# Score operands of a pair's first entry loaded in one transfer, and the issue time of a transfer counted in the list schedule

## The chip, the cores and the metric

The kernel runs on one core of one Trainium2 chip. The time is what the device takes for one execution, in microseconds (us), and lower is better. TensorE does the matrix products, VectorE, ScalarE and GpSimd the elementwise work (PE, DVE, ACT and POOL in the rows), and SyncE (SP) issues every transfer between HBM and SBUF.

## The reference

Three stages follow one another, all in float32:

```python
# attention: q, k, v are [4, 8, 576, 64]
scores = scale * np.matmul(q, k.transpose(0, 1, 3, 2))
mask = block_i >= block_j                 # blocks of 64 positions
scores = np.where(mask, scores, -1000000000.0)
scores = scores - np.max(scores, axis=-1, keepdims=True)
attn = np.exp(scores)
attn = attn / (np.sum(attn, axis=-1, keepdims=True) + 1e-09)
attn_out = np.matmul(attn, v)
x = attn_out.transpose(0, 2, 1, 3).reshape(2304, 512)
# first feed-forward, w1..w3 [512, 768], w_out [768, 512]
x = np.maximum(np.maximum(x @ w1, x @ w2), x @ w3) @ w_out
# second, w_in [512, 2048], w_out [2048, 512]
h = np.maximum(x @ w_in, 0.0)
return h * h @ w_out
```

## The kernel before

**Work and tiles.** Two heads of a batch entry make a pair, so there are 16 pairs of which the first `NPAIR` = 4 are batch entry 0. The 576 queries of a pair are cut into two groups, `GROUPS = ((0, 256), (256, 320))`. For the first four pairs the group 0 entries (256 queries, 256 keys) are done first, all four pairs, then the group 1 entries. An entry goes: score matmuls `sc` from the query tile and the key tile, the block mask and row maximum `nm` on DVE, the exponential `P` with its row sum on ACT, transposes `tp`, copies `ta`/`tb`, matmuls with `v` (`av`), row sums `r`, and the split of the result into a high and a low part (`xh`, `xl`) from which the feed-forward multiplies in three products. For the first entries the score operands are float32: for pair n a tile `zk` of 128 partitions x 3 x 256, made of two zero-padded query planes (one per head, from `in_z`) and the keys (from `in_k`). The tag `tb` of `zk` has two buffers, so the third pair's `zk` takes the buffer of the first.

**Weights.** Weight chunks of 128 x 512 float64 words come in as `raw_w`, `raw_wo`, `raw_wi` (512 KB each). ACT, DVE and POOL turn each into float32 and split it into a high and a low part (`w1h`/`w1l`, `wo1h`/`wo1l`, `wos`, and `wq` out of `wqf`). For the last feed-forward the kernel writes prepared weights back to HBM (`wo_d`, `wq_d`) and loads them again per pass (`wol`/`woh`, `wq`); `ys` tiles are written to `y_d` and come back as `yf`. In the last stage `up` makes seven products per step in two banks (`ph_x`, `ph_y`, six matmuls each), ACT copies the first of them out as `p`, DVE forms `c`, ACT and DVE split it into `g`, and `down` adds into six banks (`acc`), nine matmuls for each `g`.

**What sets the order.** Nothing is issued as the code is read. `Plan.note` records each operation with its dependences and a rank, and `Plan.issue` is a list scheduler: for each engine it keeps a time at which it is free, takes the operation that can start earliest (lowest rank first), gives it a length from `duration` or `transfer`, and emits it. The order on every engine, SP's included, comes out of those modelled times; on the chip each engine then runs its list in that order and waits in it. All emitted instructions carry the line of `Plan.call`, L187. `Plan.issue` runs twice: once for attention, the first feed-forward of the early batches and the preparation of `wo_d`, and once for the rest.

**The model's cost of a transfer.** An instruction on SP made SP busy for 60 ns, and its transfer ended at a modelled queue time plus 400 ns.

**Names.** `score_operands_f32` loads the score operands of an entry, `prefetch` calls it, and `kernel` lays out the arrays in HBM. The profile names a transfer by its tile and its source, as `zk<-in_z`.

## Time and profile before

| | us |
|---|---|
| median of 3 runs (lowest to highest) | 888.12 (883.44 to 889.05) |
| the profiled execution | 888.7 |
| its span, first to last instruction | 886.9 |
| PE busy | 864.2 (97% of the span) |
| DVE busy | 601.1 (68%) |
| ACT busy | 424.9 (48%) |
| POOL busy | 104.0 (12%) |

The profiled execution is one run, 0.6 us above the median, and 1.8 us of it lie outside the span. Busy times are shares of the whole span, over stages with different limits; a row of a timeline gives the start, the length, the engine, the operation with its tile and sources, and in brackets how long the engine stood idle ahead of it and what released it.

### The profile page before, as it was taken

The numbers are of one execution on the slowest core, as the hardware profiler recorded it, in microseconds if no ns is written. First come the engines' busy times: TensorE is split into PE (matmuls) and PEld (weight loads), VectorE is DVE, ScalarE is ACT, GpSimd is POOL, SyncE is SP. The second block draws the span as 40 slices with busy tenths as digits, with TensorE's granted clock in tenths as the row PEclk, the third lists the DMA queues.
The fourth block names the chain that finished last, engine by engine and source line by source line (L and its number), as shares of the span: only waits on it lengthen the run. The fifth ranks groups of instructions, "written<-read, shape, count | busy, mean of one in ns | idle before, by whom it ended". The sixth has DMA issues, their size and how long they took to land.

```text
span 886.9 us, 14852 instructions
## 1 busy us (share of the span) xinstructions
PE 864.2 (97%) x5464; PEld 777.7 (88%) x5464; DVE 601.1 (68%) x1376; ACT 424.9 (48%) x1016; POOL 104.0 (12%) x94
## 2 busy tenths in 40 slices
PE   5899999999999999999999989999999999999997
PEld 4567799998999989899999979898999989999896
DVE  6998678878788988646557766546755457544543
ACT  6888667667688787544555231113211114211111
POOL 2233200000001111214442230000000000000000
PEclk9999999999999999999999999999999999999999
DMA  8745432232255563554656578454765536655221
GB/s 294 237 138 174 131 114 89 85 115 86 85 184 177 175 213 118 196 190 165 257 203 237 164 299 338 160 230 168 270 229 184 207 145 229 215 200 196 72 72 71
DMA packets 52056, 157.73 MB, mean 178 GB/s; under 512 B 8592, under 2 KB 16016, under 8 KB 48400
## 3 DMA queue, kind: packets, MB, share of 16 engines
q1 hardware_dynamic: 51984, 156.78, 50.5%
q8 instruction: 43, 0.70, 0.3%
q14 instruction: 29, 0.24, 0.1%
HBM read 124.26 MB, written 32.51 MB: 177 GB/s over the span
## 4 chain that ended last, share of the span: by engine, by line
PE 92%; DVE 2%; DMA 2%; ACT 2%; issue 0%; POOL 0%; SPq 0%; ACTq 0%; POOLq 0%; DVEq 0%
PE l L187 34%; PE acc L187 22%; PE ph_x L187 11%; PE ph_y L187 8%; PE av L187 5%; PE sc L187 5%; PE tp L187 4%; PE sc_t L187 2%; DMA raw_wi<-in_win 1%; PE tp_t L187 1%; DMA raw_wo<-in_wo 1%; DMA zk<-in_k 1%; PE r L187 0%; ACT P L187 0%; DVE f_wo L187 0%
## 5 line engine op out<-in xcount | busy, mean ns | idle before, releaser
L187 PE MATMUL acc<-woh,g 128*128 128x512 f32 x576 | 198.5, 395 | 0.0
L187 PE MATMUL l<-xh,w1l 128*128 128x256 f32 (+1 forms) x576 | 174.3, 303 | 0.9 <-DVE run L187 0.9
L187 PE MATMUL l<-xl,w1h 128*128 128x256 f32 (+1 forms) x576 | 172.2, 299 | 0.0
L187 PE MATMUL l<-xh,w1h 128*128 128x256 f32 (+1 forms) x576 | 172.2, 299 | 0.0
L187 ACT CAST g<-c 128x384 fp32r<-128x384 f32 x96 | 49.3, 513 | 220.8 <-DVE c L187 220.8
L187 PEld LDWEIGHTS acc<-woh,g 128*128 128x128 f32 x576 | 108.5, 189 | 19.4
L187 PE MATMUL acc<-wol,g 128*128 128x512 f32 x288 | 113.3, 393 | 0.0
L187 PEld LDWEIGHTS l<-xh,w1l 128*128 128x128 f32 x576 | 109.0, 189 | 4.1 <-issue 1.5
L187 PEld LDWEIGHTS l<-xl,w1h 128*128 128x128 f32 x576 | 109.1, 189 | 2.6 <-issue 1.7
L187 PEld LDWEIGHTS l<-xh,w1h 128*128 128x128 f32 x576 | 109.1, 189 | 1.9 <-issue 1.2
L187 PE MATMUL ph_x<-t,wq 128*128 128x384 f32 x432 | 87.7, 337 | 2.7 <-ACT p L187 2.7
L187 PEld LDWEIGHTS ph_x<-t,wq 128*128 128x128 f32 x432 | 77.4, 188 | 8.9 <-ACT p L187 3.1
L187 DVE TENSOR_TENSOR g<-c,g 128x384 fp32r<-128x384 f32 x96 | 53.6, 560 | 43.0 <-ACT g L187 42.6
L187 ACT ACTIVATE P<-sc,nm 128x128 f32<-128x128 f32 (+3 forms) x128 | 66.9, 530 | 9.9 <-DVE nm L187 8.4
L187 DVE TENSOR_TENSOR run<-l,run 128x256 f32<-128x256 f32 (+1 forms) x96 | 43.7, 455 | 27.9 <-PE l L187 26.3
L187 POOL TENSOR_TENSOR f_wo<-f_wo,raw_wo 128x512 int32<-128x512 int32 x22 | 29.8, 1357 | 276.5 <-DVE sm L187 180.3
L187 PEld LDWEIGHTS acc<-wol,g 128*128 128x128 f32 x288 | 54.3, 189 | 7.8
L187 PE MATMUL l<-hh,wo1l 128*128 128x256 f32 (+1 forms) x192 | 57.7, 306 | 2.2 <-DVE wo1l L187 2.1
L187 PE MATMUL ph_y<-b,wq 128*128 128x384 f32 x288 | 58.3, 337 | 0.0
L187 PE MATMUL l<-hl,wo1h 128*128 128x256 f32 (+1 forms) x192 | 57.5, 301 | 0.0
L187 PE MATMUL l<-hh,wo1h 128*128 128x256 f32 (+1 forms) x192 | 57.4, 300 | 0.0
L187 DVE TENSOR_REDUCE nm<-sc 128x2 f32<-128x256 f32 (+2 forms) x96 | 55.1, 588 | 0.8
(135 smaller groups left out, 1613.1 us busy)
## 6 DMA issues: line engine op xcount, KB each, us to landing
wq<-wq_d SPq DMA_DIRECT2D x20, 1792.0 KB, 8.6
wq_d<-wq SPq DMA_DIRECT2D x8, 1792.0 KB, 7.7
raw<-in_qk SPq DMA_DIRECT2D x24, 576.0 KB, 3.8
wol<-wo_d SPq DMA_DIRECT2D x48, 256.0 KB, 3.2
woh<-wo_d SPq DMA_DIRECT2D x48, 256.0 KB, 4.8
raw_wo<-in_wo SPq DMA_DIRECT2D x22, 512.0 KB, 3.8
raw_w<-in_w SPq DMA_DIRECT2D x18, 512.0 KB, 5.0
wo_d<-wos SPq DMA_DIRECT2D x16, 512.0 KB, 3.1
```

The source lines that it names most:

```text
L187: return getattr(engine, op_name)(*map(value, args), **{k: value(x) for k, x in kw.items()})
```

## The change

Two things change. The three transfers of a first entry's score operands (`z` of head 0, `k`, `z` of head 1; 128 KB each) become one transfer of 384 KB from a new array `zk0` that `kernel` lays out in the tile's own order, for each of the four first pairs; before, the sources were rows of 1 KB, now they are rows of 3 KB. In the scheduler, issuing a transfer now holds SP for 430 ns in place of 60, and a transfer that starts in the first 6 us of the modelled time is counted 1.4 times as long. The number of transfers falls by eight; no arithmetic changes.

```diff
--- before.py
+++ after.py
@@ -264,9 +264,9 @@
                 held[e] = t + length - HOLD[e]
             for other in op.engines:
                 del waiting[other][i]
-            if e == "sp":
-                queue = max(t + 1500, queue) + transfer(op)
-                op.end, free[e] = queue + 400, t + 60
+            if op.name == "dma_start":
+                queue = max(t + 1500, queue) + transfer(op) * (1.4 if t < 6000 else 1)
+                op.end, free[e] = queue + 400, t + 430
             else:
                 op.end = t + length
                 free[e] = op.end - LAP[e]
@@ -345,7 +345,7 @@
 
 
 @with_exitstack
-def fused_kernel(ctx: ExitStack, tc: tile.TileContext, z0, k0, qk, v, w123, wo1, win2, wo2, out):
+def fused_kernel(ctx: ExitStack, tc: tile.TileContext, z0, zk0, k0, qk, v, w123, wo1, win2, wo2, out):
     nc = Plan(tc)
     mm = nc.tensor.matmul
 
@@ -493,9 +493,12 @@
         else:
             z = [at.tile([128, w], F32, tag=t, bufs=CFG["QB"][2 * (t == "kl")], name=f"z{n}_{t}") for t in ("qs", "kl")]
             k = at.tile([128, S], F32, tag="kh", bufs=CFG["QB"][1], name=f"k{n}")
-        nc.sync.dma_start(out=z[0], in_=z0[n, :, 0, a:a + w])
-        nc.sync.dma_start(out=k, in_=k0[n, :, :a + w])
-        nc.sync.dma_start(out=z[1], in_=z0[n, :, 1, a:a + w])
+        if n < NPAIR and g == 0:
+            nc.sync.dma_start(out=zk, in_=zk0[n])
+        else:
+            nc.sync.dma_start(out=z[0], in_=z0[n, :, 0, a:a + w])
+            nc.sync.dma_start(out=k, in_=k0[n, :, :a + w])
+            nc.sync.dma_start(out=z[1], in_=z0[n, :, 1, a:a + w])
         return [[(z[h], k)] for h in range(2)], None
 
     def value_operands(n, g):
@@ -1020,6 +1023,8 @@
         z0[:, h, :, h] = qn[:, h]
     z0, k0 = z0.reshape(PAIRS, 128, 2, S), kn.reshape(PAIRS, 128, S)
 
+    zk0 = np.stack([z0[:NPAIR, :, 0, :GA], z0[:NPAIR, :, 1, :GA], k0[:NPAIR, :, :GA]], axis=2)
+
     qk = np.stack([a.transpose(0, 2, 1, 3) for a in (qn, kn)], axis=3)
     qk = np.concatenate([qk, qk], axis=1)
 
@@ -1035,7 +1040,7 @@
     w123 = w123.reshape(NC1, 128, 3 * KC * 128)
     win2 = w["moe2_w_in"].reshape(KC, 128, NC2, 128).transpose(2, 1, 0, 3).reshape(NC2, 128, KC * 128)
     arrays = {
-        "z0": z0, "k0": k0, "qk": qk, "v": vc, "w123": w123, "wo1": w["moe_w_out"], "win2": win2, "wo2": w["moe2_w_out"],
+        "z0": z0, "zk0": zk0, "k0": k0, "qk": qk, "v": vc, "w123": w123, "wo1": w["moe_w_out"], "win2": win2, "wo2": w["moe2_w_out"],
     }
     arrays = {f"in_{n}": np.ascontiguousarray(a) for n, a in arrays.items()}
```

Since the scheduler's times changed, the instructions on all engines come in another order. Below, L187 is the line all have and the number behind a name counts tiles in the program, so it differs between the versions.

On ACT, at the very start, the float exponentials `P` of the first pair and the first pass over the first weight chunk `raw_w_0_0`. Before:

```order
L187 ACTIVATE raw_w_0_0_86<-raw_w_0_0_86 128x512
L187 ACTIVATE P_0_0_138,sm_0_139<-sc_0_0_120,nm_0_127 128x128 x2
L187 ACTIVATE P_1_0_149,sm_0_139<-sc_1_0_122,nm_1_135 128x256 x2
L187 ACTIVATE raw_w_0_0_86<-raw_w_0_0_86 128x512
L187 ACTIVATE raw_w_0_1_94<-raw_w_0_1_94 128x512
L187 COPY ta_158<-tp_1_0_161 128x2x256
L187 ACTIVATE raw_w_0_1_94<-raw_w_0_1_94 128x512
L187 CAST w1h_188<-raw_w_0_0_86 128x512
```

and now:

```order
L187 ACTIVATE P_0_0_119,sm_0_120<-sc_0_0_100,nm_0_110 128x128 x2
L187 ACTIVATE raw_w_0_0_84<-raw_w_0_0_84 128x512
L187 ACTIVATE P_1_0_135,sm_0_120<-sc_1_0_105,nm_1_122 128x256 x2
L187 ACTIVATE raw_w_0_0_84<-raw_w_0_0_84 128x512
L187 COPY ta_143<-tp_1_0_148 128x2x256
L187 COPY rs_0_172<-r_0_165 128x256
L187 CAST w1h_174<-raw_w_0_0_84 128x512
L187 ACTIVATE P_0_0_186,sm_0_187<-sc_0_0_151,nm_0_162 128x128 x2
```

The first pair's first exponentials (`P_0_0`) moved ahead of the weight chunk, and the second pair's (`P_0_0_186`) ahead of the second weight chunk.

On SP, the loads ahead of the third pair's `zk` (`zk_129` before, `zk_124` now). Before:

```order
L187 DMA raw_w_1_1_100<-in_w 128x1024
L187 DMA z_qs<-in_z 128x320
L187 DMA k_104<-in_k 128x576
L187 DMA z_kl<-in_z 128x320
L187 DMA z_qs<-in_z 128x320
L187 DMA k_110<-in_k 128x576
L187 DMA z_kl<-in_z 128x320 x2
L187 DMA kt_116<-in_k 128x576
L187 DMA zt_118<-in_z 128x2x64
L187 DMA zk_129<-in_z 128x256
L187 DMA zk_129<-in_k 128x256
L187 DMA zk_129<-in_z 128x256
```

and now:

```order
L187 DMA raw_w_1_1_96<-in_w 128x1024
L187 DMA z_qs<-in_z 128x320
L187 DMA k_102<-in_k 128x576
L187 DMA z_kl<-in_z 128x320
L187 DMA z_qs<-in_z 128x320
L187 DMA k_116<-in_k 128x576
L187 DMA zk_124<-in_zk 128x768
L187 DMA z_kl<-in_z 128x320 x2
L187 DMA kt_137<-in_k 128x576
L187 DMA zt_141<-in_z 128x2x64
L187 DMA zk_179<-in_zk 128x768
L187 DMA v_0_189<-in_v 128x256
```

The third pair's operands moved ahead of two `z_kl` loads, `kt` and `zt`; the fourth pair's (`zk_179`) stay behind them.

On SP, near the start of the last stage, the loads of the last two weight chunks `raw_wi`, which stand behind the loads of prepared weights `wol`/`woh`. Before:

```order
L187 DMA wol_1_6701<-wo_d 128x512
L187 DMA woh_1_6705<-wo_d 128x512
L187 DMA wol_9_6708<-wo_d 128x512
L187 DMA woh_9_6712<-wo_d 128x512
L187 DMA wq_d<-wq_6387 128x3584
L187 DMA y_d<-ys_1_3_6724 128x320
L187 DMA raw_wi_6753<-in_win 128x1024
L187 DMA raw_wi_6784<-in_win 128x1024
```

now, first the rows ahead of the `wol`/`woh` loads:

```order
L187 DMA raw_wi_6374<-in_win 128x1024
L187 DMA wq_d<-wq_6372 128x3584
L187 DMA yf_0_6531<-y_d 128x2x768
L187 DMA yf_1_6612<-y_d 128x2x768
L187 DMA y_d<-ys_1_0_6645 128x320
L187 DMA y_d<-ys_1_1_6655 128x320
L187 DMA wol_0_6682<-wo_d 128x512
```

and then the rows up to the same chunks:

```order
L187 DMA woh_1_6709<-wo_d 128x512
L187 DMA wol_1_6717<-wo_d 128x512
L187 DMA y_d<-ys_1_3_6715 128x320
L187 DMA woh_9_6726<-wo_d 128x512
L187 DMA wol_9_6733<-wo_d 128x512
L187 DMA raw_wi_6738<-in_win 128x1024
L187 DMA raw_wi_6757<-in_win 128x1024
```

The 1792 KB write `wq_d<-wq` that stood two rows ahead of the chunks now stands ahead of the `yf` loads; eight `wol`/`woh` loads stand ahead of the chunks in both.

On ACT, in the same place, from the first copy `p` of the last stage to the second. Before:

```order
L187 COPY p_0_0_6737<-ph_0_x 128x384
L187 CAST g_0_0_0_6763<-c_0_00_6750 128x384
L187 CAST wq_6782<-wqf_6717 128x3x256
L187 CAST g_0_1_1_6806<-c_0_11_6794 128x384
L187 CAST wq_6782<-wqf_6717 128x4x256
L187 CAST g_0_0_1_6831<-c_0_01_6812 128x384
L187 ACTIVATE raw_wi_6753<-raw_wi_6753 128x512
L187 ACTIVATE wqf_6846<-raw_wi_6753 128x512
L187 ACTIVATE wqf_6846<-raw_wi_6784 128x512
L187 CAST g_0_1_0_6860<-c_0_10_6828 128x384
L187 COPY p_0_1_6865<-ph_1_x 128x384
```

and now:

```order
L187 COPY p_0_0_6729<-ph_0_x 128x384
L187 CAST wq_6755<-wqf_6450 128x3x256
L187 CAST g_0_0_0_6762<-c_0_00_6744 128x384
L187 CAST wq_6755<-wqf_6450 128x4x256
L187 ACTIVATE raw_wi_6738<-raw_wi_6738 128x512
L187 ACTIVATE raw_wi_6757<-raw_wi_6757 128x512
L187 CAST g_0_1_1_6807<-c_0_11_6787 128x384
L187 ACTIVATE wqf_6816<-raw_wi_6738 128x512
L187 ACTIVATE wqf_6816<-raw_wi_6757 128x512
L187 CAST g_0_0_1_6825<-c_0_01_6804 128x384
L187 CAST g_0_1_0_6842<-c_0_10_6821 128x384
L187 COPY p_0_1_6848<-ph_1_x 128x384
```

The first pass over both `raw_wi` chunks moved ahead of three of the four `g` splits of the first step; before, one split (`g_0_1_0`) and the copy `p_0_1` stood behind them.

## Rows read from the trace of the kernel before

**Rows 1.** The span in stretches: busy us of each engine, granted clock, DMA.

```profile
0.00:12.00 12.00, 6.49 (x21) 5.08 (x22) 4.06 (x13) 4.97 (x13) 1.99 (x7) 1.00 0.82 273
12.00:25.00 13.00, 8.42 (x59) 5.33 (x57) 12.11 (x28) 10.63 (x27) 4.21 (x3) 1.00 0.96 319
25.00:50.00 25.00, 22.94 (x159) 14.94 (x159) 24.53 (x68) 23.21 (x65) 8.26 (x6) 1.00 0.70 224
...
100.00:110.00 10.00, 8.19 (x65) 7.02 (x60) 6.28 (x12) 4.93 (x10) 1.30 (x1) 0.87 0.38 122
110.00:350.00 240.00, 240.00 (x1809) 217.49 (x1809) 197.45 (x597) 178.40 (x499) 10.74 (x8) 1.00 0.41 132
...
515.00:520.00 5.00, 2.30 (x12) 1.69 (x11) 1.71 (x4) 3.17 (x6) 0.02 (x1) 1.00 1.05 442
520.00:525.00 5.00, 5.00 (x19) 4.38 (x18) 3.50 (x7) 0.97 (x3) 4.16 (x4) 0.66 0.50 182
```

**Rows 2.** Timeline of PE, first 24 us: the waits for `zk`.

```profile
3.51 2.90 PE L187 MATMUL sc<-zk 128*128 128x128 f32 x8 [3.51 <-DMA zk<-in_k]
8.41 1.62 PE L187 MATMUL sc<-zk 128*128 128x128 f32 x4 [2.00 <-DMA zk<-in_k]
...
20.63 2.86 PE L187 MATMUL sc<-zk 128*128 128x128 f32 x16 [1.96 <-DMA zk<-in_k]
```

**Rows 3.** Timeline of all engines, first 9 us: DVE's `nm`, ACT's first work.

```profile
6.59 0.15 DVE L187 TENSOR_SCALAR nm<-nm 128x2 f32<-128x2 f32 x1
...
7.57 0.66 ACT L187 ACTIVATE raw_w<-raw_w 128x512 f32<-128x512 f32 x1 [5.35 <-DMA raw_w<-in_w]
...
8.14 0.35 ACT L187 ACTIVATE P<-sc,nm 128x128 f32<-128x128 f32 x1
```

**Rows 4.** Issue to landing, first pair's third `zk` (issued 1.65 us).

```profile
DMA to landing us min/median/max: 2.7/2.7/2.7
```

**Rows 5.** Issue to landing, third pair's keys (issued 16.84 us).

```profile
DMA to landing us min/median/max: 3.7/3.7/3.7
```

**Rows 6.** Timeline of POOL, then DVE, then PE, around 103 to 107 us.

```profile
103.40 1.30 POOL L187 TENSOR_TENSOR f_wo<-f_wo,raw_wo 128x512 int32<-128x512 int32 x1 [3.61 <-DVE f_wo L187]
...
105.38 0.69 DVE L187 TENSOR_TENSOR wo1l<-f_wo,wo1h 128x512 fp32r<-128x512 f32 x1 [0.82 <-ACT wo1h L187]
...
106.13 0.39 PE L187 MATMUL l<-hh,wo1l 128*128 128x256 f32 x1 [1.71 <-DVE wo1l L187]
```

**Rows 7.** Timeline of SP, from 505 us.

```profile
505.08 0.38 SPq L187 DMA_DIRECT2D wq_d<-wq  x1
...
506.26 2.02 SPq L187 DMA_DIRECT2D raw_wi<-in_win  x2
```

**Rows 8.** Timeline of PE, 501 to 520 us.

```profile
501.71 1.20 PE L187 MATMUL ph_x<-b,wq 128*128 128x384 f32 x6
502.75 1.20 PE L187 MATMUL ph_y<-b,wq 128*128 128x384 f32 x6
...
515.27 0.39 PE L187 MATMUL acc<-woh,g 128*128 128x512 f32 x1
515.50 0.40 PE L187 MATMUL acc<-wol,g 128*128 128x512 f32 x1
...
519.52 1.50 PE L187 MATMUL ph_x<-t,wq 128*128 128x384 f32 x6 [2.70 <-ACT p L187]
```

**Rows 9.** Timeline of ACT, 516 us.

```profile
516.67 0.65 ACT L187 ACTIVATE raw_wi<-raw_wi 128x512 int32<-128x512 uint32 x1 [4.05 <-DMA raw_wi<-in_win]
```

**Rows 10.** Issue to landing of the second `raw_wi` (issued 507.9 us).

```profile
DMA to landing us min/median/max: 10.1/10.1/10.1
```

**Rows 11.** All DMA issues of `raw_wi`: count, KB, median us to landing.

```profile
raw_wi<-in_win SPq DMA_DIRECT2D x16, 512.0 KB, 5.1
```

**Rows 12.** Page, costliest groups: the split of `g` on ACT and DVE.

```profile
L187 ACT CAST g<-c 128x384 fp32r<-128x384 f32 x96 | 49.3, 513 | 220.8 <-DVE c L187 220.8
L187 DVE TENSOR_TENSOR g<-c,g 128x384 fp32r<-128x384 f32 x96 | 53.6, 560 | 43.0 <-ACT g L187 42.6
```

## The prediction

> **What bounds the kernel now.** I read the span in stretches first [rows 1]. PE is busy 864.2 of 886.9 us, so all that any reordering can give back is 22.7 us of PE idle time and what a lowered clock costs. The stretches say where that is. From 110 to 350 us PE is busy in every one of 240 us. The idle time lies in the first 50 us (5.5 of 12, 4.6 of 13, 2.1 of 25), 1.8 us after 100 us, and 2.7 us after 515 us; the tail of the span and smaller waits hold the rest. After two of these waits the granted clock is not full: 0.87 from 100 to 110 us and 0.66 from 520 to 525 us, so part of those stretches ran at 1.2 in place of 2.4 GHz. At these shares that is 10 x 0.13 = 1.3 us and 5 x 0.34 = 1.7 us of lost work.
>
> Then the timelines, to see what each wait stood for. PE waited three times for `zk`: 3.51 us at the start, 2.00 us for the second pair, 1.96 us for the third [rows 2]. The wait after 100 us is for the last weight chunk of the first feed-forward: POOL's add at 103.40, DVE's `wo1l` at 105.38, PE at 106.13 after 1.71 us [rows 6]. The wait of 2.70 us that ends at 519.52 is put down to ACT's copy `p` [rows 8], and ACT itself had stood 4.05 us in front of a `raw_wi` chunk that landed at 516.67 [rows 9].
>
> One more thing is in the stretches: DVE is busy 12.11 of 13 and 24.53 of 25 us between 12 and 50 us [rows 1]. So in the first stage PE can't run ahead of DVE for long, and a faster load is worth only what lets DVE (and ACT, 23.21 of 25) start earlier.
>
> **Term 1, fewer transfers.** Eight issues of about 0.43 us go, 3.4 us of SP time. I cost this at nothing: between 12 and 25 us the DMA engines are busy 0.96 of the time [rows 1], so an earlier issue only queues earlier. If that cover were gone, at most the 0.9 us per pair would show.
>
> **Term 2, the first scores.** PE now waits for the whole tile in place of two thirds of it. The third transfer was issued at 1.65 us and landed 2.7 us later [rows 4], at 4.35, so the first matmul can move from 3.51 to at most 4.35 us, 0.8 us later. Against that, both heads of the first score tile now come ahead of the larger one, which finishes that tile after two of the four products in place of three, about a quarter of 2.90 us or 0.7 us sooner [rows 2]. I book 0.1 us later. The larger effect is on ACT. Before, its first work was a pass over the weight chunk, which landed at 7.57 us, and the first exponential followed at 8.14 us although its bias was ready at 6.59 + 0.15 = 6.74 us [rows 3]. Now the exponential goes first. That is 8.14 - 6.74 = 1.4 us, less 0.1, so 1.3 us earlier for all that hangs on the first pair.
>
> The Trainium skill speaks against this term: "DMA: Bandwidth & Descriptors", section "Anatomy of one DMA", says that a transfer signals only when its last byte has landed, after some 2.0 us fixed and the bytes at 436 GB/s. It writes this of transfers issued by GpSimd; here SP issues. By it, as an estimate, the third 128 KB add 0.3 us to the 3.51 us at which two thirds had landed, the first matmul starts at 3.8 us, and term 2 would be 1.8 in place of 1.3 us. The row's 4.35 us decides.
>
> **Term 3, the third pair.** Its operands move ahead of two loads of 160, one of 288 and one of 64 KB, together 672 KB or 688,000 bytes. At 319 GB/s [rows 1] that is 2.2 us. The keys landed 3.7 us after their issue at 16.84 [rows 5], at 20.54, and PE started at 20.63 after 1.96 us of waiting [rows 2]; that wait is then gone. What is late next is DVE and ACT: the mask, maximum and exponentials of the third and fourth pair share them with five weight chunks. So the terms 2 and 3 don't add up, the lead that DVE gets is the limit. Bounds: nothing (or 0.8 us lost, if the tile lands late and the order gives nothing back) and 2.00 + 1.96 = 4.0 us, PE's whole waiting for the second and third pair. I take 1.5 us, nearest to term 2, because DVE is full behind it.
>
> **Term 4, the wait for `wo1l` after 100 us.** Its chain runs over POOL, ACT and DVE, which stand in the same order in both versions there. The whole first stage moves 1.5 us forward with it, and the wait of 1.71 us and the 1.3 us of lowered clock stay. I book 0, bounds -3.0 us (it closes) and +1.5 us (PE arrives early, the weights don't).
>
> **Term 5, the start of the last stage.** Here the list on ACT changes for the worse. PE needs the second split (`g_0_1_1`) for its `acc` matmuls, and ACT now makes it behind both `raw_wi` chunks. When does PE ask? Seven products at 502.75 - 501.71 = 1.04 us and nine `acc` matmuls at 515.50 - 515.27 = 0.23 us [rows 8] after 501.71: 501.71 + 7.3 + 2.1 = 511.1 us, on the old clock of events. When does the second chunk land? It is now issued at the place in SP's list (the eleventh behind the first `wol`) that the first chunk had before, 506.26 us [rows 7]. Before, the second chunk took 10.1 us to land [rows 10], with the 1792 KB write `wq_d` issued at 505.08 ahead of it [rows 7]; the median over all 16 chunks is 5.1 us [rows 11]. The write is gone from there now: 1.84 MB at 442 GB/s, the rate from 515 to 520 us [rows 1], are 4.2 us, so 10.1 - 4.2 = 5.9 us and the chunk lands at 512.2. Behind it stand ACT's pass of 0.65 us [rows 9], the split of 0.51 on ACT and 0.56 on DVE [rows 12], together 1.7 us: PE goes on at 513.9 and has waited 2.8 us. Before it waited 2.70. So a wait of the same size, 5 us sooner in the stage and for another tile, and the lowered clock after it again. I book 0; bounds by the landing time: 5.1 us gives a wait of 2.0 us (0.7 us gained), 10.1 us gives 7.0 us (4.3 us lost).
>
> **Term 6, everything between.** PE's list has the same matmuls, and the stretch 110 to 350 us has no wait to lose [rows 1]. A new one can only cost. I book 0, up to +2 us.
>
> **The sum.** The profiled execution took 888.7 us. 888.7 - 1.5 + 0 + 0 + 0 = 887.2 us. That execution lies 0.6 us above the median of the three runs, so in terms of medians I say 886.6 us.
>
> **Rivals.** (a) The lead is lost again. If the weights and not the scores set the pace up to 106 us, PE only waits longer at `wo1l`: 888.7 us in that execution, 888.1 as a median. For it speaks that ACT and DVE are full from 25 to 50 us; against it that the weight chunks go through the same two engines, which start earlier. This is also the case in which the change doesn't do what it says, because the load is bounded by the DMA engines and not by issuing. Chance 0.20.
>
> (b) Slower: ACT stands in front of `raw_wi`. One place, the start of the last stage; it decides whether the second chunk lands before or after 511.1 - 1.7 = 509.4 us. If it takes 10.1 us as before, PE waits 7.0 in place of 2.7 us: 888.7 - 1.5 + 4.3 = 891.5, as a median 890.9 us. For it speaks the order on ACT, against it the write that went away. Chance 0.14.
>
> (c) The waits close. If both the `wo1l` wait and the last stage's wait go, with their clock, that is 1.7 + 1.3 + 2.7 + 1.7 = 7.4 us, and with the lead 888.7 - 8.9 = 879.8, as a median 879.2 us; one of the two alone gives 882 to 884 us. Against it: nothing in the orders takes the chains apart. Chance 0.12.
>
> (d) Transfers cost their fixed time one by one. If each wait for `zk` was made of such times, the 4.0 us of waiting for the second and third pair would go whole, 884.7, as a median 884.1 us. What the rows show is one landing close behind the other. The Trainium skill's 2.0 us per transfer (the same section of "DMA: Bandwidth & Descriptors") would point this way. Chance 0.04.
>
> (e) New waits of over 9 us in the middle stage, from orders that nobody has run: chance 0.05, 897 us or more.
>
> **How the numbers follow.** My forecast keeps 0.45. A measurement of this kernel can tell about 1% from no change, 8.9 us. Faster by more than that needs nearly all of (c): 0.08, with something for a gain that I don't see. Slower by more needs (e) or (b) together with a new wait: 0.08. The range reaches from (c) with one wait and a half closed, 880.5, to (b) with a small new wait, 893 us.
>
> **What the profile will show.** Term 2: ACT's first exponential near 6.8 us, ahead of the first chunk. Term 3: no PE wait of 2 us for the third pair, and the `l` matmuls start 1 to 2 us sooner. Term 4: a PE wait of 1 to 2 us at `wo1l`, near 103 us. Term 5: PE's wait stands in front of `acc` with `g` and not in front of `ph_x`, 2 to 3 us long, and ahead of it ACT waits for `raw_wi`. The prediction is wrong if the wait at the start of the last stage is over 5 us or gone, if the wait at `wo1l` is gone, or if PE waits over 2 us in a place where it didn't.

## The result and the profile after

The changed kernel takes 893.65 us (median of 7 runs, 890.80 to 895.73), the kernel before in the same comparison 885.96 us (7 runs, 883.44 to 889.05). The ratio is 1.0083, with a 95% interval of 1.0061 to 1.0104: slower by 0.8%, 7.7 us between the medians. The forecast was 886.6 us with a range up to 893.0. Four of the executions behind the tables below took 950 to 4670 us; the medians count them and the ratios leave them out.

The profiled execution of the changed kernel took 893.9 us (span 892.1), the one of before 888.7. So the two traces show 5.2 of the 7.7 us; the profiled execution of before lay 2.7 us above its median. Where the 5.2 us are is read from three places.

**The first stage.** PE's waits in the changed kernel, summed by what they wait for (us in total, times, longest):

```profile
PE tp L187 <- ACT P L187: 8.1, 4, 4.8
PE acc L187 <- DVE g L187: 4.4, 1, 4.4
PE sc L187 <- DMA zk<-in_zk: 4.1, 1, 4.1
...
PE sc L187 <- ACT ys L187: 1.3, 1, 1.3
```

PE waits for `zk` only once; the waits for the second and third pair are gone. In their place stand 4.8 us for an exponential. PE's timeline of the changed kernel shows where:

```profile
4.10 2.93 PE L187 MATMUL sc<-zk 128*128 128x128 f32 x8 [4.10 <-DMA zk<-in_zk]
...
19.12 2.39 PE L187 MATMUL sc<-zk 128*128 128x128 f32 x8
...
26.30 0.48 PE L187 MATMUL tp<-ident,P 128*128 128x128 f32 x1 [4.79 <-ACT P L187]
26.56 1.06 PE L187 MATMUL sc<-zk 128*128 128x128 f32 x4
```

The third pair's scores start at 19.12 us without a wait, 1.5 us ahead of before [rows 2]. But there the matmuls at 20.63 were sixteen in a row, the scores of the third and the fourth pair together. Now eight run, and then PE's list has the third pair's first transpose ahead of the fourth pair's scores, and it waits 4.79 us for that pair's exponential. DVE's timeline of the changed kernel says what made the exponential late:

```profile
20.82 0.68 DVE L187 SCALAR_TENSOR_TENSOR f_w<-raw_w,f_w 128x512 int32<-128x512 int32 x1
21.42 0.42 DVE L187 TENSOR_TENSOR xl<-av,xh 128x256 fp32r<-128x256 f32 x1
21.75 1.44 DVE L187 TENSOR_SCALAR f_w<-f_w 128x512 int32<-128x512 int32 x1
23.23 0.69 DVE L187 SCALAR_TENSOR_TENSOR f_w<-raw_w,f_w 128x512 int32<-128x512 int32 x1
23.84 0.68 DVE L187 TENSOR_TENSOR w1l<-f_w,w1h 128x512 fp32r<-128x512 f32 x1
24.54 0.17 DVE L187 MEMSET sc<- 64x128 f32 x1
24.74 0.42 DVE L187 TENSOR_REDUCE nm<-sc 128x2 f32<-128x256 f32 x1
```

The scores were there near 21.5 us (19.12 + 2.39). DVE worked on weight chunks (and on one split `xl`) until 24.5 us, because these stood first in its list, and only then on the mask and the maximum.

Before, the exponential came hardly sooner. PE before, the same transpose and the first matmul `l` of the feed-forward:

```profile
25.77 0.68 PE L187 MATMUL tp<-ident,P 128*128 128x128 f32 x2 [1.63 <-ACT P L187]
...
27.29 0.36 PE L187 MATMUL l<-xh,w1l 128*128 128x256 f32 x1
```

and of the changed kernel:

```profile
31.84 0.36 PE L187 MATMUL l<-xh,w1l 128*128 128x256 f32 x1
```

The transpose moved from 25.77 to 26.30 us, the `l` matmul from 27.29 to 31.84. What is later is what PE still had to do behind the wait, the fourth pair's scores above all, and at which clock it did it.

The span in stretches, changed kernel (length, busy us and instructions of PE, PEld, DVE, ACT, POOL, then the granted clock, the DMA share and GB/s):

```profile
12.00:25.00 13.00, 6.51 (x38) 4.48 (x34) 12.62 (x23) 9.71 (x24) 5.12 (x4) 0.84 1.01 357
25.00:50.00 25.00, 23.32 (x142) 16.78 (x143) 21.31 (x59) 20.50 (x57) 7.85 (x6) 0.88 0.50 160
26.30:31.80 5.50, 5.50 (x17) 4.11 (x18) 3.89 (x14) 4.04 (x16) 0.00 (x0) 0.57 0.52 152
100.00:110.00 10.00, 8.26 (x72) 7.33 (x71) 8.03 (x17) 6.09 (x14) 2.58 (x2) 0.98 0.46 145
110.00:125.00 15.00, 13.69 (x89) 12.73 (x89) 10.23 (x31) 9.07 (x27) 0.00 (x0) 0.79 0.24 76
520.00:525.00 5.00, 5.00 (x22) 4.52 (x21) 3.38 (x8) 1.21 (x3) 2.48 (x2) 0.74 0.95 384
```

From 12 to 50 us the granted clock is 0.84 and 0.88 where before it was 1.00 [rows 1]: around the long wait a part of PE's work runs at 1.2 in place of 2.4 GHz, and from 26.3 to 31.8 us, behind it, most of it (0.57). One pair of traces may overstate the difference: before_order_one, below, has before's order and a clock of 0.87 and 0.93 in the same two stretches. PE gets past the wait for `wo1l` at 109.44 us, 3.3 us later than before [rows 6]. So in these two traces 1.5 us of lead at 19 us became 3.3 us of delay at 109: 4.8 us were lost in between.

**The middle.** PE, changed kernel:

```profile
109.44 0.48 PE L187 MATMUL l<-hh,wo1l 128*128 128x256 f32 x1 [1.74 <-DVE wo1l L187]
...
112.30 0.77 PE L187 MATMUL sc<-kh,qs 128*128 128x128 f32 x2 [1.31 <-ACT ys L187]
```

The wait for `wo1l` is as long as before (1.74 against 1.71 us). Behind it is a new one of 1.31 us, for a copy `ys` that stands in ACT's list behind an operand that ACT itself waits 2.02 us for. ACT, changed kernel:

```profile
110.69 0.68 ACT L187 ACTIVATE qs<-raw 128x576 fp32r<-128x576 f32 x1 [2.02 <-DMA raw<-in_qk]
111.28 0.65 ACT L187 CAST kh<-raw 128x576 fp32r<-128x576 f32 x1
111.84 0.64 ACT L187 COPY ys<-l 128x256 f32<-128x256 f32 x2
```

The lowered clock now falls behind 110 us (0.98, then 0.79). The last stage begins at 505.36 us (its first `ph_x` matmul) against 501.71 [rows 8], 3.65 us later, of which 3.3 came from the first stage; so in this pair of traces nearly all that was lost here is given back before 505 us (the traces put together at the end of the experiments show more).

**The last stage.** PE, changed kernel:

```profile
519.26 0.80 PE L187 MATMUL acc<-woh,g 128*128 128x512 f32 x1 [4.36 <-DVE g L187]
```

ACT, changed kernel, ahead of that:

```profile
516.33 0.65 ACT L187 ACTIVATE raw_wi<-raw_wi 128x512 int32<-128x512 uint32 x1 [5.97 <-DMA raw_wi<-in_win]
517.57 0.65 ACT L187 ACTIVATE raw_wi<-raw_wi 128x512 int32<-128x512 uint32 x1 [0.58 <-DMA raw_wi<-in_win]
518.12 0.49 ACT L187 CAST g<-c 128x384 fp32r<-128x384 f32 x1
```

Here PE waits in front of `acc`, not of `ph_x`, for a split `g` that ACT makes behind both weight chunks. This wait is 4.36 us where before had 2.70 [rows 8], and with the clock behind it the stage costs 1.5 us more. 3.3 + 0.35 + 1.5 make the 5.2 us of these two traces.

### The profile page after: what moved, and what is told of

It is laid out like the page before. It is cut to its first block, busy times and chain, and to the rows that moved or that the text cites. A ratio compares the mean times of both kernels' runs of the same rounds, so it can differ in the third digit from the quotient of the medians.

```text
span 892.1 us, 14831 instructions
## 1 busy us (share of the span) xinstructions
PE 866.0 (97%) x5464; PEld 779.7 (87%) x5464; DVE 607.2 (68%) x1378; ACT 422.1 (47%) x1014; POOL 104.0 (12%) x94
## 4 chain that ended last, share of the span: by engine, by line
PE 92%; DMA 3%; DVE 2%; ACT 1%; issue 0%; POOL 0%; SPq 0%; ACTq 0%; POOLq 0%; DVEq 0%
PE l L187 33%; PE acc L187 22%; PE ph_x L187 11%; PE ph_y L187 8%; PE sc L187 5%; PE av L187 5%; PE tp L187 4%; PE sc_t L187 2%; DMA raw_wi<-in_win 1%; PE tp_t L187 1%; PE r L187 1%; DMA raw<-in_qk 1%; DMA woh<-wo_d 0%; DMA raw_w<-in_w 0%; DMA raw_wo<-in_wo 0%
## 5 line engine op out<-in xcount | busy, mean ns | idle before, releaser
L187 PE MATMUL acc<-woh,g 128*128 128x512 f32 x576 | 197.9, 394 | 4.4 <-DVE g L187 4.4
L187 PE MATMUL l<-xh,w1l 128*128 128x256 f32 (+1 forms) x576 | 173.1, 301 | 0.0
L187 PE MATMUL l<-xl,w1h 128*128 128x256 f32 (+1 forms) x576 | 172.7, 300 | 0.0
L187 PE MATMUL l<-xh,w1h 128*128 128x256 f32 (+1 forms) x576 | 172.7, 300 | 0.0
L187 ACT CAST g<-c 128x384 fp32r<-128x384 f32 x96 | 49.3, 513 | 220.5 <-DVE c L187 220.5
L187 PEld LDWEIGHTS acc<-woh,g 128*128 128x128 f32 x576 | 108.3, 188 | 24.1 <-DVE g L187 4.8
L187 PE MATMUL acc<-wol,g 128*128 128x512 f32 x288 | 113.3, 393 | 0.0
L187 PEld LDWEIGHTS l<-xh,w1l 128*128 128x128 f32 x576 | 108.9, 189 | 4.3 <-issue 2.7
L187 PEld LDWEIGHTS l<-xl,w1h 128*128 128x128 f32 x576 | 109.0, 189 | 1.5 <-issue 0.9
L187 PEld LDWEIGHTS l<-xh,w1h 128*128 128x128 f32 x576 | 109.1, 189 | 1.2 <-issue 0.7
L187 PE MATMUL ph_x<-t,wq 128*128 128x384 f32 x432 | 87.4, 337 | 0.0
L187 DVE TENSOR_TENSOR g<-c,g 128x384 fp32r<-128x384 f32 x96 | 53.3, 557 | 46.7 <-ACT g L187 46.0
L187 PEld LDWEIGHTS ph_x<-t,wq 128*128 128x128 f32 x432 | 77.4, 188 | 5.8
L187 ACT ACTIVATE P<-sc,nm 128x128 f32<-128x128 f32 (+3 forms) x128 | 67.0, 531 | 16.7 <-DVE nm L187 15.5
L187 DVE TENSOR_TENSOR run<-l,run 128x256 f32<-128x256 f32 (+1 forms) x96 | 43.6, 454 | 30.5 <-PE l L187 29.7
L187 PEld LDWEIGHTS acc<-wol,g 128*128 128x128 f32 x288 | 54.3, 189 | 7.9
L187 POOL TENSOR_TENSOR f_wo<-f_wo,raw_wo 128x512 int32<-128x512 int32 x22 | 28.8, 1311 | 277.2 <-DVE nm_t L187 159.3
L187 PE MATMUL tp<-ident,P 128*128 128x128 f32 x320 | 53.1, 278 | 8.1 <-ACT P L187 8.1
L187 PE MATMUL l<-hh,wo1l 128*128 128x256 f32 (+1 forms) x192 | 57.9, 304 | 1.7 <-DVE wo1l L187 1.7
L187 PE MATMUL l<-hl,wo1h 128*128 128x256 f32 (+1 forms) x192 | 58.3, 304 | 0.1
L187 PE MATMUL ph_y<-b,wq 128*128 128x384 f32 x288 | 58.3, 337 | 0.0
L187 PE MATMUL l<-hh,wo1h 128*128 128x256 f32 (+1 forms) x192 | 58.1, 303 | 0.0
```

Of the source, the lines that this page charges most:

```text
L187: return getattr(engine, op_name)(*map(value, args), **{k: value(x) for k, x in kw.items()})
```

## Experiments

The theory is that the order which the scheduler made is the cause. The rivals are that the large transfer itself is (it lands as a whole), or that only one of the three places is. All medians stand here; the texts below use the ratios. A ratio is taken from runs of before in the same rounds, whose medians went from 885.96 to 887.13 us, so it is not exactly a quotient of two medians of this table.

| kernel | median us | ratio to before | 95% interval |
|---|---|---|---|
| changed | 893.65 | 1.0083 | 1.0061 to 1.0104 |
| before_order_one | 886.88 | 1.0006 | 0.9990 to 1.0022 |
| after_order_three | 895.46 | 1.0097 | 1.0070 to 1.0123 |
| swap_start | 894.15 | 1.0082 | 1.0056 to 1.0109 |
| swap_last | 890.88 | 1.0036 | 1.0018 to 1.0054 |
| merge_only | 888.82 | 1.0035 | 1.0017 to 1.0053 |
| costs_only | 891.29 | 1.0058 | 1.0037 to 1.0080 |
| swap_all | 888.04 | 1.0023 | 1.0009 to 1.0037 |
| before_one_last | 886.14 | 1.0005 | 0.9984 to 1.0026 |
| start_dve | 893.83 | 1.0085 | 1.0063 to 1.0106 |
| all_dve | 890.04 | 1.0029 | 1.0017 to 1.0041 |
| before_one_last2 | 885.41 | 0.9985 | 0.9970 to 1.0001 |
| fill_start | 892.55 | 1.0062 | 1.0041 to 1.0082 |
| fill_all | 886.91 | 1.0006 | 0.9990 to 1.0022 |

### The transfer without the order, and the order without the transfer

**before_order_one** emits the order of the kernel before, instruction for instruction, with one transfer at the place of the first of three.

```diff
+        if n < NPAIR and g == 0:
+            load[0].parts, load[1].parts, load[2].parts = [(zk, zk0[n])], [], []
...
-            self.tc.keep_in_program_order(self.call(self.real[e], alias(e, op.name), op.args, op.kw))
+            for kw in [op.kw] if op.parts is None else [dict(out=o, in_=i) for o, i in op.parts]:
+                self.tc.keep_in_program_order(self.call(self.real[e], alias(e, op.name), op.args, kw))
```

> Every instruction in the order of before; only the score operands of the first four pairs come in one transfer each, at the place of the first of the three. Theory 1 (the loss lies in the new order): the first scores start near 4.1 us in place of 3.51, everything else stays, median within 1.5 us of before, 884.5 to 887.5. Theory 2 (the merged transfer itself is what costs): 889 us or more.

**after_order_three** is the reverse: the changed kernel's order, with three transfers at the place of the one.

```diff
-            nc.sync.dma_start(out=zk, in_=zk0[n])
+            load = nc.sync.dma_start(out=zk, in_=zk0[n])
+            load.parts = [(z[0], z0[n, :, 0, a:a + w]), (k, k0[n, :, :a + w]), (z[1], z0[n, :, 1, a:a + w])]
```

> Every instruction in the order of after; each merged transfer is three again, one behind the other at the same place. Theory 1 (order): as slow as after, 891.5 to 895 us, with the PE wait of about 4.8 us at 26 us and that of about 4.4 us at the start of the last stage still there. Theory 2 (transfer): back near before, 888 us or less.

With before's order the merged transfer costs and gives nothing (1.0006). With the new order three transfers are as slow as one, if not slower (1.0097 against 1.0083, the intervals overlap). PE's longest waits in after_order_three are in the same places as in the changed kernel:

```profile
PE tp L187 <- ACT P L187: 7.9, 4, 4.5
...
PE sc L187 <- DMA zk<-in_k: 3.4, 1, 3.4
PE acc L187 <- DVE g L187: 3.4, 1, 3.4
```

So the order is the cause, and the transfer itself is not. The wait for `g` is 3.4 us here and 3.2 to 3.9 us in swap_start, start_dve and fill_start, whose lists are the changed kernel's at that place; the 4.36 us above are the longest of the five.

### Which edit made the order

**merge_only** has the new transfer and the old lines of the scheduler, **costs_only** the new lines and three transfers, each scheduled anew.

```diff
 merge_only, against the changed kernel; costs_only is this reversed, against before
-            if op.name == "dma_start":
-                queue = max(t + 1500, queue) + transfer(op) * (1.4 if t < 6000 else 1)
-                op.end, free[e] = queue + 400, t + 430
+            if e == "sp":
+                queue = max(t + 1500, queue) + transfer(op)
+                op.end, free[e] = queue + 400, t + 60
```

> One transfer for the score operands of a first entry, and the scheduler's old cost of a transfer (60 ns of SP, no factor of 1.4). Its list has the fourth pair's scores ahead of the third pair's transposes, the copies ys ahead of the load qs, and in the last stage the copy p and three of the four splits g ahead of the chunks raw_wi. Theory 1 (the new cost of issuing makes the orders that lose time, and the merged transfer loses none): faster than before, 881 to 885 us, with no PE wait over 2 us behind 12 us. Rival (the transfer set free early is what upsets the order, whatever its cost): 890 us or more.

> Three transfers as before, and the scheduler's new cost of a transfer. Its list has the third pair's transposes wholly ahead of the fourth pair's scores, and in the last stage both raw_wi passes ahead of three splits g, as after has. Theory 1 (the cost makes the losing orders): as slow as after or slower, 892 to 897 us. Rival (as above): 888 us or less.

Either alone makes it slower. costs_only (1.0058) waits in the changed kernel's three places, in the first of them in six pieces of at most 1.6 us and not in one of 4.8. PE's waits of costs_only, by what they wait for:

```profile
PE tp L187 <- ACT P L187: 5.6, 6, 1.6
PE acc L187 <- DVE g L187: 2.7, 1, 2.7
PE sc L187 <- ACT ys L187: 1.6, 1, 1.6
```

merge_only (1.0035) was expected to gain and missed. Its last-stage wait is 0.2 us, but PE waits 3.71 us for an exponential at 26.84 us, and it has a long wait in a new place. PE of merge_only:

```profile
398.37 0.64 PE L187 MATMUL l<-xh,w1l 128*128 128x320 f32 x1 [3.87 <-ACT run L187]
```

ACT of merge_only, same place:

```profile
397.38 0.62 ACT L187 CAST wos<-f_wo 128x512 fp32r<-128x512 f32 x1 [3.45 <-DMA wo_d<-wos]
397.90 0.42 ACT L187 COPY run<-l 128x320 f32<-128x320 f32 x1
```

ACT stands in front of the one buffer `wos`, whose last contents were still on their way to HBM, with the copy `run` that PE needs behind it. A small edit of eight transfers at the start re-dealt the list 380 us later. A version with that wait repaired was not tried.

### The places one by one

The next kernels keep the scheduler's order but for a few instructions. Emission goes into a list, and `later` takes the operations that match `move`, with those that depend on them, behind the last one that matches `behind`:

```diff
-            self.tc.keep_in_program_order(self.call(self.real[e], alias(e, op.name), op.args, op.kw))
+            order.append(op)
...
+        for move, behind in MOVES:
+            order = later(order, move, behind)
+        for op in order:
+            self.tc.keep_in_program_order(self.call(self.real[op.engine], alias(op.engine, op.name), op.args, op.kw))
```

**swap_start** puts the fourth pair's scores ahead of the third pair's transposes on PE, as before had them:

```diff
+MOVES = [(lambda op: "tp2_0_0" in tiles(op, True), lambda op: op.engine == "pe" and "sc3_1_0" in tiles(op, True))]
```

> After, with one exchange in PE's list: the first transposes of the third pair stand behind the fourth pair's scores. All other lists are unchanged. Theory 1 (PE stood 4.79 us in front of that transpose with the fourth pair's scores behind it): the fourth pair's scores run from 21.5 us, the wait falls to about 2 us, the first feed-forward product moves from 31.84 to about 28.5 us, and the time falls by 2 to 4 us to about 890.5. Rival (DVE, full of weight chunks, sets the pace anyway): the first feed-forward product moves by less than 1 us and the time stays at 893. Second rival: the lead is there at 32 us and lost again at the wait for the last weight chunk near 104 us.

The time did not move (1.0082 against 1.0083). PE of swap_start:

```profile
18.54 4.06 PE L208 MATMUL sc<-zk 128*128 128x128 f32 x16
...
25.74 0.68 PE L208 MATMUL tp<-ident,P 128*128 128x128 f32 x2 [3.15 <-ACT P L208]
```

The sixteen scores are together again, and the wait only shrank from 4.79 to 3.15 us: DVE's list still sets the exponential. The first `l` matmul came at 29.37 in place of 31.84 us and the `wo1l` wait ended 1.6 us sooner, at 107.85; the interval of this ratio is too wide to tell so small a gain from none.

**start_dve** also takes the weight-chunk work on DVE behind the third pair's exponentials:

```diff
+    (lambda op: op.engine == "dve" and {"f_w1_1_1", "w1l1"} & {*tiles(op, True)}, lambda op: op.engine == "act" and "P2_1_0" in tiles(op, True)),
```

> After, with the exchange of swap_start (PE's transpose of the third pair behind the fourth pair's scores) and one on DVE: four operations on the weight chunks move from ahead of the third pair's masks and maxima to behind them. Theory 1 (the third pair's P was late because DVE made chunks first): DVE's nm of the third pair moves from 24.7 to about 22 us, PE's wait in front of the transpose falls from 4.8 and 3.1 us to under 1.5, and the first feed-forward product moves to 27 or 28 us, about where before had it. The stretch near 112 us is unchanged, so 889 to 891 us if the lead lasts. Rival (the chunks moved back make the products themselves wait, or the lead is lost at the last weight chunk near 107 us): 893 us.

PE of start_dve:

```profile
24.39 0.68 PE L209 MATMUL tp<-ident,P 128*128 128x128 f32 x2 [1.40 <-ACT P L209]
...
30.87 0.66 PE L209 MATMUL r<-ident,sm 128*64 128x128 f32 x8 [3.64 <-DVE sm L209]
```

The wait for the exponential is down to 1.40 us, and one of 3.64 us for the row sums `sm` has come up behind it, on the same engine. The first `l` matmul is at 26.64 us, ahead of before's 27.29, and yet the `wo1l` wait ends at 109.21, 3.1 us behind before's. No gain (1.0085): DVE has this work to do whichever comes first, and the wait moves.

**swap_last** takes ACT's first pass over both `raw_wi` chunks behind the copy `p0_1` of the last stage:

```diff
+    (lambda op: op.engine == "act" and {f"raw_wi_3", f"raw_wi_{3 + NQ}"} & {*tiles(op, False)},
+     lambda op: op.engine == "act" and "p1_0_1" in tiles(op, True)),
```

> After, with one exchange in ACT's list: the four passes over the last two weight chunks raw_wi stand behind the four splits of the first step and the copy p of the second; nothing else moves but one DVE operation on the chunk. Theory 1 (ACT stood in front of the chunks with g behind them): PE's wait of 4.4 us for g goes and the lowered clock after it (0.74 from 520 to 525 us, 1.3 us) with it, 888 us, at most 890. Rival (the wait only moves on, to the next product or to the weights made of the chunks): a new PE wait of 2 to 3 us behind 515 us and 891 to 892 us.

PE of swap_last:

```profile
517.17 0.50 PE L209 MATMUL acc<-woh,g 128*128 128x512 f32 x1 [0.50 <-DVE g L209]
```

The wait of 4.36 us is down to 0.50, and the clock from 520 to 525 us is 1.00. The ratio fell from 1.0083 to 1.0036, 0.47% or 4.2 us. Before has a wait of that kind too, so this is not all of the change's making.

**swap_all** has the moves of swap_start and swap_last, and in the middle the `ys` copy ahead of ACT's wait for the operand, with the scores behind the matmuls that do not need them:

```diff
+    (lambda op: op.engine == "act" and "raw4_1" in tiles(op, False), lambda op: op.engine == "act" and "ys0_0_1" in tiles(op, True)),
+    (lambda op: op.engine == "pe" and {"sc4_0_0", "sc4_1_0"} & {*tiles(op, True)} and {"kh_4_1", "kl_4_1"} & {*tiles(op, False)},
+     lambda op: op.engine == "pe" and "l2_0_0_2" in tiles(op, True)),
```

> After, with three exchanges: the one at the start (PE's transpose of the third pair behind the fourth pair's scores), the one of the last stage (ACT's raw_wi passes behind the splits and the second copy p), and a third near 112 us: ACT's qs and kh of one transfer behind the two ys copies, and PE's four score products from them behind the third group of l products. Theory 1 (three places of an unlucky order make up the loss, and each is worth its wait and the lowered clock after it): about 1 us from the start, 2.5 us from the middle (wait 1.3 us, and 3.4 us more than before at the lower clock), 4.5 us from the last stage, in all 884 to 887 us. Rival (each gain is given back at the next wait): 889 us or more.

**all_dve** is swap_all with the move of start_dve added (its diff is that line).

> The same two exchanges at the start, and those near 112 us and of the last stage as in swap_all. Theory 1: 2 to 3 us less than swap_all (888.0), 885 to 886 us, as fast as before or a little faster. Rival (as in start_dve): 888 us.

In swap_all the `ys` wait is gone. The clock from 110 to 125 us is 0.89 in place of 0.79, but swap_last, which keeps a `ys` wait of 2.0 us, has 0.89 there too. The ratio, 1.0023, is 0.13% or 1.2 us under swap_last's, with overlapping intervals. all_dve (1.0029) again gains nothing from DVE's order. What is left is in the first stage, by the table at the end of the experiments.

### Before's last stage

If the last stage is worth 4.2 us in the new order, before should gain as well. **before_one_last** is before_order_one with the move of swap_last; **before_one_last2** moves the chunks behind DVE's last `g` of that step too:

```diff
-     lambda op: op.engine == "act" and "p1_0_1" in tiles(op, True)),
+     lambda op: op.engine == "act" and "p1_0_1" in tiles(op, True) or op.engine == "dve" and "g0_0_1_0" in tiles(op, True)),
```

> The order of before, one transfer for the operands, and ACT's passes over the last raw_wi chunks behind the last split of the first step and the second copy p. Theory 1: PE's wait of 2.2 to 2.7 us for p and the lowered clock after it go, 3 to 4.4 us less than before, 882 to 884 us. Rival (the wait moves on to the weights made of these chunks or to the next transfers): 885.5 to 887.5 us.

> before_one_last, and DVE's two first operations on the last raw_wi chunks also behind its split of the fourth g. In before_one_last PE waited 2.3 us for that split, because DVE stood in front of the chunk in ACT's place. Theory 1: this wait goes, 1.5 to 2.5 us less, 883.5 to 884.5 us, the fastest of all. Rival (the weights made of these chunks are the next to be late): 886 us.

The first gained nothing (1.0005). DVE of before_one_last:

```profile
517.65 0.43 DVE L209 TENSOR_SCALAR wqf<-wqf 128x512 int32<-128x512 int32 x1 [4.06 <-ACT wqf L209]
...
519.28 0.55 DVE L209 TENSOR_TENSOR g<-c,g 128x384 fp32r<-128x384 f32 x1
```

Now DVE stands 4.06 us in front of the next pass over the chunk, with the `g` that PE needs behind it, and PE still waits 2.33 us. With that moved too, the stretch from 515 to 520 us is full; before_one_last2:

```profile
515.00:520.00 5.00, 4.95 (x25) 4.08 (x23) 2.49 (x6) 3.36 (x6) 0.00 (x0) 1.00 1.05 443
```

Its median is the lowest of all, but 0.9985 with an interval up to 1.0001 is not told apart from before.

### The clock

**fill_start** is the changed kernel's order with 36 transposes of the identity, 4 us of work that nobody uses, in PE's 4.8 us wait; they write the bank that the next transpose overwrites. **fill_all** is the same with the moves of the middle and of swap_last.

```diff
+            if op.engine == "pe" and "tp2_0_0" in tiles(op, True) and not self.filled:
+                self.filled = True
+                bank, _, ident = op.args
+                for _ in range(36):
+                    self.tc.keep_in_program_order(self.call(self.real["pe"], "transpose", (bank, ident, ident), {}))
```

> After, with 36 transposes of the identity put into PE's list ahead of the third pair's first transpose, into the bank that this transpose then overwrites. They take some 4 us of PE in the place of its wait of 4.8 us and do nothing else; no other list changes. Theory A (the start loses its time by the lower granted clock after the long wait: over the profiles so far, the later the first stage ends, the lower the clock from 12 to 50 us, from 1.00 in before to 0.87 in after): the clock from 12 to 50 us rises from 0.87 to 0.95 or more, the wait for the last weight chunk ends near 107 in place of 109.4 us, and the time falls by 2 to 3 us to about 891. Theory B (the clock is only a sign of the waiting, and the order of chunks and masks on DVE and ACT sets the end of the stage): the clock rises, the end of the stage stays near 109.4 us, and the time stays at 893 to 894.

> The 36 filling transposes, and the exchanges near 112 us and of the last stage as in swap_all; the start's own order is that of after. Theory A: as swap_all or 1 to 2 us less, 886 to 888 us. Theory B: 888 to 890 us.

PE of fill_start:

```profile
23.07 4.09 PE L206 MATMUL tp<-ident 128*128 128x128 f32 x36
...
27.73 0.33 PE L206 MATMUL tp<-ident,P 128*128 128x128 f32 x1 [0.57 <-ACT P L206]
```

The stretch from 25 to 50 us of fill_start:

```profile
25.00:50.00 25.00, 24.05 (x168) 17.66 (x168) 23.57 (x64) 21.74 (x61) 8.83 (x6) 1.00 0.59 187
```

The clock of that stretch is 1.00 in place of 0.88. (The stretch from 12 to 25 us has 0.87, much as in the changed kernel.) From the start of the third pair's scores to the end of the `wo1l` wait it takes 88.45 us (108.95 - 20.50), against 90.32 (109.44 - 19.12) in the changed kernel and 85.50 (106.13 - 20.63) before [rows 2, 6]. The gain lies behind the wait. PE of fill_start at the first `l` matmul:

```profile
30.97 0.36 PE L206 MATMUL l<-xh,w1l 128*128 128x256 f32 x1
```

and the stretch ahead of it:

```profile
27.70:30.90 3.20, 3.17 (x17) 2.44 (x18) 3.13 (x10) 2.84 (x11) 0.00 (x0) 1.00 0.72 197
```

From the third pair's first transpose to the first `l` matmul PE runs the same instructions: 3.24 us in fill_start and 3.23 in fill_all, against 5.54 in the changed kernel, 5.58 in swap_last and 5.80 in after_order_three. So the lowered clock behind the wait costs some 2.3 us there.

In the whole time this is not told apart. fill_start was forecast at about 891 us if the clock costs time and at 893 to 894 if not, and took 892.55. It is 0.21% under the changed kernel (1.0062), and fill_all, which lacks swap_start's move, is 0.17% under swap_all (1.0006); the intervals overlap in both pairs. fill_all stands level with before.

One trace of a kernel says little of a stage, but traces with the same lists in a stretch can be put together (us; the last stage begins with its first `ph_x`). costs_only and merge_only, whose lists are their own, are not in this table, and after_order_three counts with the changed order:

| order in the stretch | third pair's scores to the end of the `wo1l` wait | to the last stage | to the end |
|---|---|---|---|
| before's | 85.20, 85.50, 88.29, 88.32 | 393.28 to 395.81 (4 traces) | 383.16, 385.19 |
| changed | 90.32, 90.59, 90.97 | 395.43 to 397.25 (6) | 385.71 to 387.50 (5) |
| changed, with the move made there | swap_start's 88.83, 89.31; start_dve's 90.27, 90.36; filled 88.23, 88.45 | 393.56 to 394.71 (3) | 382.25 to 382.83 (4) |

By the means, the changed order costs 3.8 us in the first stage, 1.6 in the middle and 2.2 in the last; the third pair's scores start about 0.5 us sooner, so this is about 7 of the 7.7 us. Before's order has two kinds of first stage in its four traces. In before and before_one_last (85.50, 85.20) PE waits at most 1.63 us for the third pair's exponentials, and the clock from 26 to 30 us is 1.00. In before_order_one and before_one_last2 (88.29, 88.32) it waits 2.98 and 3.59 us, and that clock is 0.59 and 0.57. So with the wait filled, the changed order takes as long as before's slower kind, and 3 us longer than its faster one.

## Why the prediction was wrong

Of the three signs that it named for being wrong, one came: PE waits over 2 us in a place where it didn't, at 26.30 us. The wait at the last stage stayed under 5 us, and the one for `wo1l` is still there. As a change, -1.5 us was forecast and +7.7 measured. The prediction also held that a measurement tells about 1% from no change; the interval came out at 0.2% to either side, so 0.8% is told apart.

**The step that failed is term 3**, "I take 1.5 us". The operands did come sooner: no wait of 2 us for the third pair, and its scores start 1.5 us earlier in this trace (0.5 us in the mean of all with one transfer and the changed lists up to there). But the `l` matmuls, forecast 1 to 2 us sooner, start 4.55 us later, and 4.8 us are lost by the `wo1l` wait, so the term came out as +3.3 us in place of -1.5, outside its bounds of +0.8 and -4.0. The table above bears this out: 90.3 to 91.0 us for that stretch in three traces, against 85.2 to 88.3 in four of before's order. I had judged the order by when operands arrive and by DVE being full, and had not read on in PE's list, where the third pair's transpose now stands ahead of the fourth pair's scores, or in DVE's, where a weight chunk stands ahead of the third pair's mask. Both could be read from the order. swap_start and start_dve show that neither is the whole cause by itself; fill_start shows a part that the term had no price for, the lowered clock behind the wait, some 2.3 us.

**Term 1** holds: before_order_one at 1.0006.

**Term 2** holds: the first exponential is at 6.35 us (6.8 forecast), the first matmul at 4.10 us (at most 4.35), and at 3.78 to 4.25 us in all twelve traces with one transfer. With three transfers it is at 3.43, 3.51 and, in costs_only, 4.29 us. The Trainium skill's sum ("DMA: Bandwidth & Descriptors", section "Anatomy of one DMA") gave 3.8 us for that matmul, as an estimate, 0.3 us less than the 4.10 us of this trace. Its rule, a signal only when all bytes have landed, would have the one large transfer land later than the second of three: 4.10 against 3.51 us agrees, the 4.29 us of costs_only does not. What the first pair's lead was worth by itself no run shows.

**Term 4** holds for the wait (1.74 us) and not for its place: I had it near 103 us, it ended at 109.44. The new wait of 1.31 us for `ys`, and the lowered clock that moved behind 110 us, were not foreseen. With that wait taken out, the middle is about 2 us shorter in the traces; in the ratios swap_all is 1.2 us under swap_last, which is not told apart.

**Term 5** had the right mechanism and place; the size was off. I took 5.9 us from issue to landing for the second chunk, and it was 7.3, issued at 510.2 us, so the wait was 4.36 and not 2.8 us and the stage cost +1.5 us in place of 0. This is rival (b)'s mechanism with less than its price. swap_last shows it as the cause of that wait: with ACT's passes moved, 0.50 us is left, and the time falls by 0.47%.

**Term 6**, booked at 0, came out at +0.35 us in the pair of traces and at 1.6 us in the means of the table, within its bound of +2.

**The rivals.** (b) was right on one place, and its 890.9 us still had the lead of 1.5 us in it. (a) said that the lead is lost again, not that it turns into a loss. (c), waits that close, did not happen. (d) had it right that PE's waits for the second and third `zk` go, and not that the time goes with them; against a fixed time for each transfer stands before_order_one. (e) put new waits in the middle, and the largest new one is in the first stage.

**Open.** What in the order of DVE and ACT makes the rest of the first stage's loss, up to 3 us against the faster kind of before even with the wait filled: two re-orderings there moved the waits and, in the time, gained nothing that can be told apart. No kernel joined swap_start's move with the filled wait. Why start_dve loses behind its first `l` matmul what it won ahead of it was followed only to the wait for `sm`. How much of swap_last's 4.2 us before pays in most of its runs: the trace of before has 2.70 us of wait and 1.7 us of clock, before_order_one has 2.20 us with the clock at 1.00, and removing it gained 0.15%, which is not told apart from nothing.

## What to carry to other kernels

A cost that feeds a list scheduler is an edit of the whole program: cost the order that comes out, engine by engine, up to the next wait of each, before what the edit was for. Where two pieces of work share a full engine, an earlier operand may give no time, and an in-order list can make another engine wait for the wrong one. Do not price a stage from one trace of each kernel: here one order gave 85.2 and 88.3 us for the same stretch, and traces with the same lists told more together. To tell an edit from the order that it causes, emit the old order with the new instruction, as before_order_one does.

## What was not expected of the hardware

Waits of like length are followed by different clocks. The stretch from 520 to 525 us, behind 2.70 us of waiting, had 0.66 before [rows 1]. Behind 2.7 us in costs_only and 2.2 us in before_order_one it had 1.00. The stretch of costs_only:

```profile
520.00:525.00 5.00, 5.00 (x28) 4.65 (x27) 4.01 (x9) 0.96 (x3) 2.49 (x2) 1.00 0.99 353
```

and of before_order_one:

```profile
520.00:525.00 5.00, 5.00 (x27) 4.46 (x26) 3.79 (x8) 1.35 (x2) 4.16 (x5) 1.00 0.35 122
```

And with useless matmuls in a wait of 4.8 us the clock behind it was 1.00 in place of 0.57, and the same work took 3.2 us in place of 5.5 to 5.8. On the whole kernel's time the two pairs show some 0.2%, with overlapping intervals.
